# Gated linear attention by half chunks on 64x64 array tiles, ahead of a routed expert layer

## The chip, the cores and the metric

The kernel runs on one core of a Trainium2 chip. A core has a matrix engine (TensorE, PE in the profile; its weight loads are listed as PEld), three engines for elementwise work (VectorE or DVE, ScalarE or ACT, GpSimd or POOL), SyncE (SP), which issues DMA transfers, and 16 DMA engines behind it. The metric is the device time of the core in microseconds, the median of the runs. TensorE multiplies a stationary operand (`lhsT`, loaded as weights) with a moving one (`rhs`) and writes to PSUM[...].

## The reference

Two stages. The first is a gated linear recurrence over 768 steps, for 4 sequences of 8 heads with 48 dimensions each:

```python
for t in range(S):
    state = alpha[:, :, t, :, None] * state + np.einsum('bhd,bhe->bhde', k[:, :, t], v[:, :, t])
    y[:, :, t] = np.einsum('bhd,bhde->bhe', q[:, :, t], state)
```

Its result, as 3072 rows of 384 numbers, goes to a routed layer of 8 experts. Each row is given to the expert with the largest logit, and the result is scaled by that expert's softmax weight:

```python
logits = x @ w_gate                        # (3072, 384) @ (384, 8)
expert_idx = np.argmax(logits, axis=1)
...
h = np.maximum(x_sorted[lo:hi] @ w1[e], 0.0)   # w1[e]: (384, 1024)
y_sorted[lo:hi] = h @ w2[e]                    # w2[e]: (1024, 384)
...
return gate_w[:, None] * y
```

Everything is fp32.

## The kernel before

The recurrence is cut into 24 chunks of 128 steps (4 sequences of 6). Within a chunk the decays are turned into running sums of logarithms: with `cp = exp(cum)`, the queries become `q * cp`, the keys `k / cp`, and the chunk is a masked attention plus a product with the state that the chunk began with. Heads are handled in four pairs (`NP = 4`), each head padded from 48 to 64 (`DP`), so that a pair fills 128 partitions. A loop runs over `s`; in one pass different steps of several chunks are done:

```python
for s in range(-5, NT + 1):
    do(load, s + 8 if s + 8 >= 4 else -1, "akq")
    do(load, s + 5, "v")
    do(logs, s + 5)          # ScalarE: ln(alpha)
    do(cums, s + 4)          # TensorE: running sums; ScalarE: two exponentials
    do(operands, s + 3)      # GpSimd: k * icp, q * cp
    do(transposes, s + 2)
    ...
    do(rows, s - 1)
    do(scores, s + 1)
    do(keep_rows, s - 1)     # to the DRAM tensor x_rows
    do(decay_out, s + 3)
    do(decay_in, s + 2)
    ...                      # choice of experts for groups of chunks
    do(attend, s)
    ...                      # one-hot matrices of the routing
```

The steps that the change touches (cut):

```python
def cums(s):
    cum = ps.tile([C, Dm], F32, name="cum")
    nc.tensor.matmul(cum[:], lhsT=cmask[:], rhs=d["ln"][:], start=True, stop=True)
    ...
    nc.scalar.activation(d["icp"][:], cum[:], AF.Exp, scale=-1.0)
    nc.scalar.activation(d["cp"][:], cum[:], AF.Exp)

def decay_out(s):            # last row of cp to memory, and back as a column per head pair
    nc.scalar.dma_start(e_d[s : s + 1, :], st[s]["cp"][C - 1 : C, :])
def decay_in(s):
    for a in range(2):
        nc.scalar.dma_start(d["E"][a * DP : a * DP + D, :], ...)

def transposes(s):           # k and q, four 128x128 transposes each
    ...
        if i: nc.vector.tensor_copy(d[n][:], tp[:])      # qT
        else: nc.scalar.copy(d[n][:], tp[:])             # kT

def scores(s):
    for p in range(NP):
        for t, r in ((sA, 0), (sB, DP)):
            nc.tensor.matmul(t[:, p, :], lhsT=d["kT"][r : r + D, p, :], rhs=d["qT"][r : r + D, p, :], ...)
    nc.vector.tensor_tensor(d["dA"][:], sA[:], cmask..., op=ALU.mult)
    nc.scalar.copy(d["dB"][:], sB[:])
    nc.gpsimd.affine_select(d["dB"][:], d["dB"][:], ...)  # mask of the second head

def attend(s):
    y = ps.tile([C, NP, C], F32, name="y")
    if c > 0:                # state of the chunk before
        ... nc.tensor.matmul(y[r : r + DP, p, :], lhsT=st[s - 1]["U"][r : r + D, p, :], rhs=d["qT"][...], ...)
    for p in range(NP):
        for i, r in enumerate((0, DP)):
            nc.tensor.matmul(y[r : r + DP, p, :], lhsT=d["v"][:, 2 * p + i, :], rhs=d["d" + "AB"[i]][:, p, :], ...)
    if c + 1 < NB:           # k^T v of the chunk
        ... nc.tensor.matmul(kv[r : r + DP, p, :], lhsT=kqb[s % 4][:, 0, 2 * p + i, :], rhs=d["v"][...], ...)
    nc.vector.tensor_copy(d["yT"][:], y[:])
    # U = (kv + U before) * decay of the chunk: VectorE adds, GpSimd multiplies

def rows(s):                 # back to rows; `back` holds an identity and the gate's weights
    for p in range(NP):
        nc.tensor.matmul(xr[:, p, :], lhsT=d["yT"][:, p, :], rhs=back[:, p, :], start=True, stop=True)
    nc.vector.reduce_sum(lgn[:, s, :], ...)
def keep_rows(s):
    xs = work.tile([C, W], F32, name="xs")               # two buffers
    nc.scalar.copy(xs[:, :Dm]..., d["xr"][:, :, :D2])
    nc.gpsimd.tensor_copy(xs[:, Dm:], lgn[:, s, :])
    nc.sync.dma_start(x_d[s * C : (s + 1) * C, :], xs[:])
```

After the loop the last rows are routed, rows are gathered by expert from `x_rows`, and the expert layer runs (not changed but for the time at which weights are fetched). The weights of expert 0 are fetched in pass 15, those of experts 1 and 2 when the expert stage begins.

Of the kernel before, what the change touches and what calls it, by code (L numbers as in the profile page):

```python
# [8 lines left out]
F32 = mybir.dt.float32  # L9
# [9 lines left out]
def kernel(  # L19
# [10 lines left out]
):  # L30

# [42 lines left out]

    consts = ctx.enter_context(tc.tile_pool(name="consts", bufs=1))
    ident = consts.tile([C, C], F32)
    cmask = consts.tile([C, C], F32)
    back = consts.tile([C, NP, D2 + E], F32)
    kqb = [consts.tile([C, 2, H, DP], F32, name=f"kqb{i}") for i in range(4)]
    vb = [consts.tile([C, H, DP], F32, name=f"vb{i}") for i in range(6)]  # L80
    Ub = [consts.tile([C, NP, DP], F32, name=f"Ub{i}") for i in range(2)]
    Eb = [consts.tile([C, NP], F32, name=f"Eb{i}") for i in range(5)]

    def first_consts():
# [6 lines left out]
        for t in Ub + Eb:  # L91
            nc.vector.memset(t[:], 0.0)

        for a in range(2):
            r = slice(a * DP, a * DP + D)
            nc.vector.tensor_copy(
                back[r, :, a * D : (a + 1) * D], ident[r, None, a * DP : a * DP + D].to_broadcast([D, NP, D]),
            )
            nc.vector.tensor_scalar_mul(back[r, :, D2:], back[r, :, D2:], -1.0)
# [48 lines left out]
    e_d = nc.dram_tensor("decay_rows", (NT, Dm), F32, kind="Internal").ap()  # L148
# [27 lines left out]
    with tc.tile_pool(name="ld", bufs=6) as ld, \  # L176
         tc.tile_pool(name="work", bufs=2) as work, \
         tc.tile_pool(name="ps", bufs=1, space=PSUM) as ps, \
         tc.manual_schedule():
        st = {s: {} for s in range(NT)}  # L180

# [4 lines left out]
        def load(s, names):  # L186
            for n in names:
                src = rows_of({"a": alpha, "k": k, "q": q, "v": v}[n], s)
                if n == "v":
                    st[s][n] = vb[s % len(vb)]  # L190
                    nc.sync.dma_start(st[s][n][:, :, :D], src)
                else:
                    t = ld.tile([C, H, D], F32, name=n + "_sb", bufs=4 if n == "a" else 6)
                    nc.sync.dma_start(t[:], src)  # L194
                    st[s][n] = t
# [8 lines left out]
        def heads(t):  # L204
            return t[:].rearrange("s (h d) -> s h d", h=H)

        def cums(s):
            d = st[s]
            cum = ps.tile([C, Dm], F32, name="cum")
            nc.tensor.matmul(cum[:], lhsT=cmask[:], rhs=d["ln"][:], start=True, stop=True)  # L210
            d["icp"] = work.tile([C, Dm], F32, name="icp")
            d["cp"] = work.tile([C, Dm], F32, name="cp", bufs=3)
            nc.scalar.activation(d["icp"][:], cum[:], AF.Exp, scale=-1.0)  # L213
            nc.scalar.activation(d["cp"][:], cum[:], AF.Exp)  # L214

        def decay_out(s):
            if s % NB + 1 < NB:
                nc.scalar.dma_start(e_d[s : s + 1, :], st[s]["cp"][C - 1 : C, :])

        def decay_in(s):  # L220

            d = st[s]
            if s % NB + 1 < NB:
                d["E"] = Eb[s % len(Eb)]
                for a in range(2):
                    nc.scalar.dma_start(
                        d["E"][a * DP : a * DP + D, :], e_d[s].rearrange("(p a d) -> a d p", a=2, d=D)[a],
                    )

        def operands(s):  # L230
            d = st[s]
            kq = kqb[s % 4]
            nc.gpsimd.tensor_tensor(kq[:, 0, :, :D], d["k"][:], heads(d["icp"]), op=ALU.mult)  # L233
# [13 lines left out]

        def scores(s):
            d = st[s]
            sA = ps.tile([C, NP, C], F32, name="sA")  # L250
            sB = ps.tile([C, NP, C], F32, name="sB")
            for p in range(NP):
                for t, r in ((sA, 0), (sB, DP)):
# [12 lines left out]
        def attend(s):  # L266
# [38 lines left out]
            for r in ranked:  # L305
                slots_of(*r)
# [357 lines left out]
```

## Time and profile before

The time is 489.24 us (median of three; 489.02 to 489.99). The profiled execution spans 488.0 us.

| group (line) | count | mean ns | what it is |
|---|---|---|---|
| PE cum (210) | 48 | 601 | running sums, two records each |
| PE tp (241) | 192 | 282 | transposes |
| PE sA, sB (254) | 192 + 192 | 285 | scores |
| PE y (274) | 320 | 275 | product with the state |
| PE y (280) | 192 + 192 | 279 | product with the values |
| PE kvp (291) | 320 | 221 | k^T v |
| PE xr (313) | 192 | 275 | back to rows |
| DVE dA, yT, qT | 24 each | 687 to 689 | mask and copies out of PSUM |
| ACT kT, dB | 24 each | 591, 588 | copies out of PSUM |
| POOL kqb (233, 234) | 24 each | 996 | operands |
| POOL dB (261) | 24 | 634 | mask of the second head |

A row of the profile's groups names the line, the engine, the operation and the tiles (written <- read). For TensorE a second pair such as 128\*64 tells how many rows and columns of the array are used, followed by the moving operand. Matmuls overlap, so the mean length of one is longer than the distance between two; a rate is read from starts in the timeline. The expert stage's two groups of matmuls (lines 528 and 553) are busy for 148.4 and 146.8 us of the span.

### The profile page before, as it was taken

The page shows a single profiled execution, that of the slowest core. Times are in us where ns is not written, and L with a number is a line of the kernel's source. Part 1 is how long each engine was busy: PE and PEld are TensorE (multiplying, and loading weights), DVE is VectorE, ACT ScalarE, POOL GpSimd, SP SyncE. Part 2 cuts the span into 40 slices and gives each one's busy share as a digit, 9 for nine tenths or more (in the row PEclk, how much of TensorE's full clock was granted, in tenths as well). Part 3 has the DMA queues.
Part 4 walks back from the last instruction along what each step waited for, and adds up shares of the span by engine and source line. Part 5 has one row for each costly group of instructions (what it writes and reads, how often), then busy time and mean ns, then how long its engine had stood idle before and what let it go on. Part 6 is the DMA issues. An engine that isn't in the chain of part 4 may idle for free.

```text
span 488.0 us, 7370 instructions
## 1 busy us (share of the span) xinstructions
PE 457.6 (94%) x2881; PEld 297.4 (61%) x2881; DVE 142.3 (29%) x391; ACT 103.2 (21%) x209; POOL 137.8 (28%) x226
## 2 busy tenths in 40 slices
PE   2999999999999389999999999999999999999992
PEld 0788888888898275555555555555555455555451
DVE  2344766665778421212401201101201201301100
ACT  3544544544421001101001111011111001101010
POOL 3556745555642270010124010016020020010020
PEclk9999999999999779999999999999999999999997
DMA  9999999889992151300726400537300040000000
GB/s 161 199 177 203 207 210 203 168 170 272 299 356 107 50 160 39 142 32 8 267 75 211 135 32 0 189 118 249 129 28 16 1 166 22 1 20 16 2 32 25
DMA packets 127213, 59.76 MB, mean 122 GB/s; under 512 B 110304, under 2 KB 121604, under 8 KB 127178
## 3 DMA queue, kind: packets, MB, share of 16 engines
q1 hardware_dynamic: 114818, 48.87, 39.6%
q0 software_dynamic: 3584, 10.34, 6.4%
q10 hardware_dynamic: 8776, 0.08, 1.0%
q8 instruction: 23, 0.38, 0.3%
q14 instruction: 12, 0.10, 0.1%
HBM read 49.70 MB, written 10.35 MB: 123 GB/s over the span
## 4 chain that ended last, share of the span: by engine, by line
issue 54%; PE 27%; POOL 11%; DVE 2%; DMA 2%; SPq 1%; ACT 0%; POOLq 0%; ACTq 0%
POOL out_dram L559 6%; POOL xg L499 5%; PE sA L254 5%; PE y L280 4%; PE tp L241 4%; PE xr L313 4%; PE cum L210 4%; PE y L274 4%; PE kvp L291 2%; SPq L194 1%; DMA a_sb<-in_alpha_dram 1%; DMA x_rows<-xs 1%; DVE yT L295 1%; DVE sc L330 0%; DVE dA L258 0%
## 5 line engine op out<-in xcount | busy, mean ns | idle before, releaser
L528 PE MATMUL hp<-xT,w 128*128 128x448 f32 (+2 forms) x402 | 148.4, 530 | 1.2 <-DVE xT L524 1.2
L553 PE MATMUL zp<-w,h_sb 128*128 128x384 f32 (+1 forms) x512 | 146.8, 488 | 0.0
L528 PEld LDWEIGHTS hp<-xT,w 128*128 128x128 f32 x402 | 77.4, 194 | 69.9 <-issue 65.0
L553 PEld LDWEIGHTS zp<-w,h_sb 128*128 128x128 f32 (+1 forms) x512 | 81.1, 177 | 62.4 <-issue 13.6
L559 POOL DMA_INDIRECT out_dram<-zo,g_idx x28 | 27.7, 988 | 251.7 <-ACT zo L558 251.7
L542 DVE TENSOR_SCALAR h_sb<-hp 128x448 f32<-128x448 f32 x32 | 20.0, 624 | 218.4 <-PE hp L528 218.4
L544 ACT ACTIVATE h_sb<-hp 128x448 f32<-128x448 f32 x32 | 17.4, 543 | 142.0 <-PE hp L528 142.0
L558 ACT ACTIVATE zo<-zp,gw 128x384 f32<-128x384 f32 x28 | 16.3, 581 | 133.6 <-PE zp L553 129.0
L210 PE MATMUL cum<-ln,cmask 128*128 128x384 f32 x48 | 24.7, 601 | 8.7 <-ACT cp L214 4.4
L499 POOL DMA_INDIRECT xg<-x_rows,g_idx x28 | 26.9, 960 | 12.2 <-issue 12.2
L241 PEld LDWEIGHTS tp<-ident,kqb 128*128 128x128 f32 x192 | 23.5, 146 | 7.9 <-issue 4.2
L254 PE MATMUL sA<-qT,kT 48*128 48x128 f32 x192 | 27.7, 285 | 0.0
L254 PE MATMUL sB<-qT,kT 48*128 48x128 f32 x192 | 27.7, 285 | 0.0
L233 POOL TENSOR_TENSOR kqb<-k_sb,icp 128x384 f32<-128x384 f32 x24 | 23.9, 996 | 8.8 <-ACT icp L213 8.6
L241 PE MATMUL tp<-ident,kqb 128*128 128x128 f32 x192 | 26.2, 282 | 0.0
L280 PE MATMUL y<-dA,vb 128*64 128x128 f32 x192 | 26.1, 279 | 0.0
L280 PE MATMUL y<-dB,vb 128*64 128x128 f32 x192 | 26.1, 279 | 0.0
L313 PE MATMUL xr<-back,yT 128*128 128x104 f32 x192 | 25.4, 275 | 0.7 <-DVE yT L295 0.5
L261 POOL TENSOR_SCALAR_AFFINE_SELECT dB<-dB 128x512 f32<-128x512 f32 x24 | 15.2, 634 | 37.3 <-ACT dB L260 23.8
L254 PEld LDWEIGHTS sA<-qT,kT 48*128 48x128 f32 x192 | 23.1, 187 | 2.6 <-issue 0.3
L313 PEld LDWEIGHTS xr<-back,yT 128*128 128x128 f32 x192 | 23.3, 192 | 1.5 <-issue 1.0
L234 POOL TENSOR_TENSOR kqb<-q_sb,cp 128x384 f32<-128x384 f32 x24 | 23.9, 996 | 0.0
(117 smaller groups left out, 403.0 us busy)
## 6 DMA issues: line engine op xcount, KB each, us to landing
w<-in_moe_w_dram SPq DMA_DIRECT2D x16, 1536.0 KB, 6.8
x_rows<-xs SPq DMA_DIRECT2D x24, 196.0 KB, 2.9
a_sb<-in_alpha_dram SPq DMA_DIRECT2D x24, 192.0 KB, 4.1
k_sb<-in_k_dram SPq DMA_DIRECT2D x24, 192.0 KB, 3.8
q_sb<-in_q_dram SPq DMA_DIRECT2D x24, 192.0 KB, 4.0
vb<-in_v_dram SPq DMA_DIRECT2D x24, 192.0 KB, 4.6
Eb<-decay_rows ACTq DMA_DIRECT2D x40, 0.8 KB, 3.0
xg<-x_rows,g_idx POOLq DMA_INDIRECT x28, 3.1
```

The source lines that it names most:

```text
L210: nc.tensor.matmul(cum[:], lhsT=cmask[:], rhs=d["ln"][:], start=True, stop=True)
L233: nc.gpsimd.tensor_tensor(kq[:, 0, :, :D], d["k"][:], heads(d["icp"]), op=ALU.mult)
L234: nc.gpsimd.tensor_tensor(kq[:, 1, :, :D], d["q"][:], heads(d["cp"]), op=ALU.mult)
L241: nc.tensor.transpose(tp[:, p, :], pair(kqb[s % 4][:, i], p), ident[:])
L254: nc.tensor.matmul(t[:, p, :], lhsT=d["kT"][r : r + D, p, :], rhs=d["qT"][r : r + D, p, :], start=True, stop=True,)
L280: nc.tensor.matmul(y[r : r + DP, p, :], lhsT=d["v"][:, 2 * p + i, :], rhs=d["d" + "AB"[i]][:, p, :], start=(c == 0 and p == 0), stop=True, ...
L313: nc.tensor.matmul(xr[:, p, :], lhsT=d["yT"][:, p, :], rhs=back[:, p, :], start=True, stop=True)
L499: nc.gpsimd.indirect_dma_start(out=xg[:, j, :], out_offset=None, in_=x_d[:, :], in_offset=bass.IndirectOffsetOnAxis(ap=i, axis=0),)
L528: nc.tensor.matmul(hp[:, c0:c1], lhsT=w1[:, a, f * C : (f + 1) * C], rhs=xT[:, a, c0:c1], start=(a == 0), stop=(a == DB - 1), skip_group_c ...
L542: nc.vector.tensor_relu(h[:, f, :cols], hp[:, :cols])
L553: nc.tensor.matmul(zp[i * m : (i + 1) * m, :], lhsT=h[:, f, c0 : c0 + m], rhs=w2[:, f, :], start=(f == 0), stop=(f == FB - 1), skip_group_ ...
L559: ins = nc.gpsimd.indirect_dma_start(out=out[:, :], out_offset=bass.IndirectOffsetOnAxis(ap=idx, axis=0), in_=zo[:], in_offset=None, bound ...
```

## The change

The chunk stays at 128 steps, but inside it each half of 64 steps (`j`) is attended by itself: scores and value products exist only within a half, and what passes from half 0 to half 1 goes through an extra state, `U[:, 1]`. All products with operands of 48 or 64 rows and 64 columns are so placed that four of them, one for each half `j` and each head `a` of a pair, sit on the four 64x64 tiles of the array; for half 1 the two heads' places in `y` are exchanged (`at(j, a)`), so that state products on different rows never meet in the same PSUM partitions of a bank. The aim is to do four small products at a time where two larger ones were done, and to leave out the block of the score square that the mask sets to zero.

```diff
+    HALVES = [(j, a) for j in range(2) for a in range(2)]
+    def at(j, a):
+        return DP * (a ^ j)
...
+        def inter(s):
+            for p in range(NP):
+                for j, a in HALVES:
+                    if j or s % NB:
+                        nc.tensor.matmul(
+                            y_ps[at(j, a) : at(j, a) + DP, j, p, :],
+                            lhsT=Ub[s % 2][head(a), j, p, :], rhs=d["qT"][head(a), p, half(j)],
+                            start=(p == 0), stop=False, skip_group_check=True,
+                        )
         def scores(s):
-                for t, r in ((sA, 0), (sB, DP)):
+                for j, a in HALVES:
                     nc.tensor.matmul(
-                        t[:, p, :], lhsT=d["kT"][r : r + D, p, :], rhs=d["qT"][r : r + D, p, :], ...
+                        sc_ps[half(j), a, p, :], lhsT=d["kT"][head(a), p, half(j)], rhs=d["qT"][head(a), p, half(j)], ...
-            nc.scalar.copy(d["dB"][:], sB[:])
-            nc.gpsimd.affine_select(d["dB"][:], ...)
+            nc.vector.tensor_tensor(d["dAB"][:], sc_ps, m64..., op=ALU.mult)
         def attend(s):
+            n = s + 1            # kv of the next chunk, by halves
+                        nc.tensor.matmul(kv_ps[half(a), j, p, :],
+                            lhsT=kqb[n % 4][half(j), 0, 2 * p + a, :], rhs=st[n]["v"][half(j), 2 * p + a, :D], ...)
+                    nc.tensor.matmul(y_ps[at(j, a) : at(j, a) + DP, j, p, :],
+                        lhsT=d["v"][half(j), 2 * p + a, :], rhs=d["dAB"][half(j), a, p, :], ...)
+        def state(s):            # U[:, 1] = kv of half 0 + U[:, 0];  acc = kv of half 1 + U[:, 1]
+        def decay(s):            # GpSimd: U[:, 0] of the next chunk = acc * E
+        def results(s):
+            nc.scalar.copy(st[s]["yT"][:], y_ps)
         def rows(s):
-                nc.tensor.matmul(xr[:, p, :], lhsT=d["yT"][:, p, :], rhs=back[:, p, :], ...)
+                for j in range(2):
+                    nc.tensor.matmul(xr[half(j), p, :], lhsT=d["yT"][:, j, p, :], rhs=back[:, j, p, :], ...)
```

The chunk's decay is no longer sent through memory; TensorE picks the last row of `cp` out with a column of the identity, and ScalarE copies it:

```diff
-        def decay_out(s): / decay_in(s):     # three DMA issues by ScalarE
+        def decays(s):
+            last_ps = sums_tile()[:, Dm + 4 * E : Dm + 4 * E + NP]
+            for p in range(NP):
+                for a in range(2):
+                    nc.tensor.matmul(last_ps[half(a), p : p + 1],
+                        lhsT=cpb[s % 3][DP:, h : h + DP], rhs=ident[DP:, C - 1 :], ...)
+                nc.scalar.copy(st[s]["E"][:], last_ps)
```

The loop has a new order. The transposes come ahead of the running sums, the operands and logarithms one chunk further ahead of their use, and each PSUM bank is read by one engine at a time: scores and kv by VectorE, y by ScalarE. Loads go with a fixed lookahead and five buffers each for alpha, k and q; the store of rows stands at the head of the following pass.

```diff
+        for s in range(-5, NT):
+            do(store_rows, s - 1)
+            loads(s)             # v of s + 5, k and q of s + 7, alpha of s + 8
+            if s + 1 >= 0: attend(s)
+            do(state, s + 1)
+            ... decay(s + 1)
+            do(decays, s + 2)
+            do(results, s)
+            ... # ranking products
+            do(transposes, s + 2)
+            do(cums, s + 4)
+            do(operands, s + 4)
+            do(inter, s + 1)
+            do(scores, s + 2)
+            ... # one-hot matrices
+            do(rows, s)
+            do(keep_rows, s)
+            ... # choice of experts
+            do(logs, s + 5)
+            if s in (NT - 7, NT - 4):
+                e = (s - NT + 7) // 3
+                w_t[e] = fetch1(e), fetch2(e)
...
-        w_t[1] = fetch1(1), fetch2(1)      # at the start of the expert stage
```

So the weights of expert 0 are fetched in pass 17 and those of expert 1 in pass 20.

## The prediction

> **What bounds the kernel now.** I read the page first: the busy times and the slices.
>
> ```profile
> PE 457.6 (94%) x2881; PEld 297.4 (61%) x2881; DVE 142.3 (29%) x391; ACT 103.2 (21%) x209; POOL 137.8 (28%) x226
> ...
> PE   2999999999999389999999999999999999999992
> DMA  9999999889992151300726400537300040000000
> ```
>
> TensorE is full but for the start and one hole at slices 14 and 15. The hole is the border of two stages: attention up to about 164 us, the expert products from 170 us to the end. The diff touches the expert stage only in when weights are fetched, so its 318 us stay. What is to be won lies in the first 164 us, and there the DMA row is near 9 as well: a second resource stands close behind TensorE.
>
> Next the chain of waits in order of time, for one chunk in the middle. Columns: start, length (us), work.
>
> ```profile
> 65.65 0.84 PE cum L210 x2
> 66.50 0.87 PE tp L241 x8
> 67.37 0.87 PE xr L313 x8
> 69.33 1.02 PE y L274 x16
> 70.35 1.02 PE y L280 x16
> 71.83 0.84 PE cum L210 x2
> ```
>
> The chain never leaves TensorE: the period is 71.83 - 65.65 = 6.18 us. The scores fill 68.24 to 69.33 (1.09) and the key-value products 71.37 to 71.83 (0.46). The sum 0.84 + 0.87 + 0.87 + 1.09 + 1.02 + 1.02 + 0.46 is 6.17, so there is no idle time. The windows view of the same chunk agrees:
>
> ```profile
> 65.65:71.83 6.18, 6.18 (x84) 5.42 (x83) 4.39 (x14) 2.84 (x6) 3.23 (x6) 1.00 1.10 225
> ```
>
> PE is busy for all 6.18 us, VectorE for 4.39, ScalarE 2.84, GpSimd 3.23; the clock is full and DMA moves 225 GB/s. Then the timeline of TensorE by form, for what one product costs.
>
> ```profile
> 70.99 0.27 PE L280 MATMUL y<-dA,vb 128*64 128x128 f32 x1
> 71.00 0.27 PE L280 MATMUL y<-dB,vb 128*64 128x128 f32 x1
> 71.10 0.27 PE L280 MATMUL y<-dA,vb 128*64 128x128 f32 x1
> 71.11 0.27 PE L280 MATMUL y<-dB,vb 128*64 128x128 f32 x1
> 71.21 0.62 PE L291 MATMUL kvp<-vb,kqb 128*64 128x48 f32 x16
> 71.76 0.91 PE L210 MATMUL cum<-ln,cmask 128*128 128x384 f32 x2
> ```
>
> Every fp32 product is two records. Two products on different column halves start 0.01 us apart: they run together, and a round of two takes 0.11 us at 128 moving columns. Kvp (64 weight columns, 48 moving) has eight rounds: its 0.62 less the last record's 0.222 (median by the tile view), over seven gaps, is 0.057 us a round. So 64 weight columns with at most 64 moving ones cost about 0.058 a round; 128 of either cost 0.109 (0.87 / 8).
>
> Last, SyncE's issues, and the chain at the end of the stage.
>
> ```profile
> 39.06 0.64 SPq L322 DMA_DIRECT2D x_rows<-xs  x1
> ...
> 58.35 0.90 SPq L322 DMA_DIRECT2D x_rows<-xs  x1
> ```
>
> Between these lie three more stores and sixteen loads: four chunks in 19.29 us, 4.82 us a chunk, while SyncE still catches up with its lookahead. That is the pace at which loads and stores can go.
>
> ```profile
> 157.75 0.69 DVE yT L295
> ...
> 166.67 1.21 POOL xg L499
> ```
>
> The routing after the last chunk is a chain of short VectorE steps and a gather; the first expert matmul starts at 170.25.
>
> [...] the y groups take 1.02 for eight rounds of 0.109 = 0.87, so a switch is 0.15, for the scores 1.09 - 0.87 = 0.22. Four tiles at once occur in no part of this trace. [...] Loads here are runs of 48 floats, 192 B, and 4.82 us for 0.98 MB (four loads of 192 KB and a store of 196) is about 204 GB/s.
>
> **The change part by part, per chunk.** A round is up to four 64x64 products side by side; each group of 16 products has 4 x 2 = 8 rounds.
> - Scores: only keys and queries of the same half are multiplied; the block between the halves is left to the state. 8 x 0.058 = 0.46 for 1.09.
> - State products (inter): 0.46 for 1.02. They now also carry half 0 into half 1 through an extra state. y from scores: 0.46 for 1.02.
> - kv: by half chunks, 32 records for 16, four tiles for two: 0.46 as before.
> - Decays: new, eight products with one moving column, two tiles: 8 x 0.058 = 0.46 added. They replace the round trip of the decay row through memory.
> - rows: 64 weight columns, 104 moving, two tiles: 8 x 0.109 x 104/128 = 0.71 for 0.87.
> - Transposes 0.87 and sums 0.84 stay; transposes first merely give ScalarE and VectorE time for their copies.
> - Switches: 64x64 to full, to 64x64, to 128x64, to 64x64: 0.15 + 0.22 + 0.15 + 0.15 = 0.67. About 0.2 of the sums' 0.84 (two passes over 384 columns at 0.109 per 128 are 0.65) was their own switch and goes.
>
> Sum: 5 x 0.46 + 0.71 + 0.87 + 0.65 + 0.67 = 5.2 us; 5.3 with the ranking products. Before, the first chunk of a sequence saved its whole state product and the last its kv; now the first still runs one half and the last one half, in as many rounds, so these shortcuts are gone. The y groups on lines 274 and 280 put chunk 0 at 21.75 and chunk 18 at 129.98, hence 6.01 a chunk on average. 18 x (6.01 - 5.3) = 12.8 us. The last five chunks took 26.6 (to 156.6); without sums, then without transposes and scores, I give them 5.3 + 5.3 + 4.5 + 4.5 + 3.2 = 22.8: 3.8 us.
>
> Other engines: ScalarE loses the dB copy (0.59) and three DMA issues (0.31 to 0.46 each), gains the yT copy (0.59) and a tiny decay copy (I take 0.2): ln 0.52, exps 0.97, kT 0.59, yT 0.59, xs 0.48, decay 0.2 are 3.4 of 5.3. VectorE loses yT (0.69), gains a 0.35 add: about 4. GpSimd loses the select (0.63). None gets to 5.3, so these changes by themselves lie beside TensorE.
>
> Start: the products of chunk 0 come in the pass that also needs alpha of chunk 4, the 15th load in the new order: 0.8 + 15 x 1.03 us a load (37 loads stood ahead of the store at 39.06) is 16.3, so I put y of chunk 0 near 17, 4.7 earlier than 21.75; ScalarE now takes the next logarithm after the exponentials, not before, and no longer stalls them on a later load. Against this stands the result buffer xs with its two copies: xs of chunk 2 needs the first store landed. That store now has 31 loads ahead of it: 0.8 + 31 x 1.03 = 32.7, plus 2.9 to land (the page's median), about 35.6. TensorE alone would want it near 17 + 3 x 5.3 = 33, so some 2.6 are lost again. Net 2 us gained. 12.8 + 3.8 + 2 = 18.6 for the stage. The routing tail keeps its length, and expert 1's weights no longer compete with the first gather: up to 0.5 us, within the error.
>
> 489.2 - 18.6 is 470.6; I put 470.
>
> **Rivals.**
> (a) Four tiles do not run at once, or TensorE's instruction stream doesn't keep up: records per chunk double from 82 to about 170. Against it: pairs start 0.01 apart and two kinds of pairs, rows and columns, both work. For it: nothing here shows more than two. If kv, y, inter and scores ran two by two, 4 x 0.46 is added: 7.1 us a chunk, 18 x 1.1 and the rest 25 us slower: about 512.
> (b) DMA becomes the bound. It needs 4.82 a chunk against 5.3, and two experts' weights (3 MB each, 3.15 MB at about 400 GB/s, some 8 us) are now pulled into the stage, against one before. They come after the last k, q and alpha loads, so I expect little; but if chunk periods stretched to 5.8, it is about 479.
> (c) ScalarE's order: kT waits behind the decay copy and yT, the next exps behind kT. Its chain inside a chunk (decays end at 1.4, then 0.2, 0.6, 0.6 and about 0.2 of latency: 3.0) is ahead of the scores (due at 3.6) by 0.6 only. If it slips, the period is 5.6 to 5.8: 475 to 479.
> (d) All goes faster: cheaper switches, no wait for xs; 5.0 a chunk, but DMA's 4.82 stops it: about 462.
>
> **Range and chances.** (d) gives the lower end with some margin, 460; (b) and (c) the upper, 481. Faster by over 2% means under 479.5. I give (a) in full or in part 9%, and 7% to a gain eaten by waits; faster 0.84.
>
> **What would show it.** Windows of one chunk: period near 5.3 and PE busy throughout. The timeline: four starts within 0.03 us, rounds of 0.058; rounds of 0.11 mean (a). The chain of waits staying on PE, else ACT kT, Eb or xs (c), or loads of alpha and x_rows (b). First y near 17 us, last near 138, expert start about 151, expert stage still 318 us. It is wrong if the four-tile rounds cost over 0.09 us, or if the expert stage moves.

## The result, and the profile after

| | median us (range, runs) | ratio to the kernel before, 95% interval |
|---|---|---|
| before | 489.18 (489.02 to 489.99) | |
| after | 505.92 (505.64 to 507.32, 4) | 1.0345 (1.0322 to 1.0367) |

The change makes the kernel 16.7 us slower; 19 us faster were predicted. The ratio leaves out executions over 1.5% above the fastest of their kernel, which the medians keep. First the page of the kernel after: busy times, the slices of TensorE, its clock and DMA, and the queue that the page lists as `instruction`.

```profile
PE 456.9 (90%) x4993; PEld 292.3 (58%) x4993; DVE 131.7 (26%) x396; ACT 106.3 (21%) x229; POOL 126.6 (25%) x206
...
PE   3899898989869649999999999999999999999993
...
PEclk9999988989989777999999999999999999999997
DMA  9999977979764925130255330255330040000000
...
q8 instruction: 40, 0.66, 0.6%
```

The same queue in the page of before (packets, MB, share):

```profile
q8 instruction: 23, 0.38, 0.3%
```

TensorE is busy for as long as before (456.9 us against 457.6) in a span that is 17.6 us longer. Where its row of before had nines, several slices of the attention stage have an 8 or a 6 now, and the clock row falls to 8 or 7 in five slices of that stage and in two behind its last y; before, it did so only at the border of the stages. (At the start the clock row has nines because the trace has no record of the clock there, not because the clock was full; see below.) Records of matrix products, two to an fp32 product, went from 2881 to 4993. The line of queue 8 was easily passed over: 40 packets of instructions for 23.

Two passes in the windows view of after. Columns: stretch, length, then busy time and count of PE, PEld, VectorE, ScalarE and GpSimd, the granted clock, the DMA share and GB/s.

```profile
70.40:75.57 5.17, 5.17 (x184) 4.39 (x180) 2.65 (x5) 2.94 (x7) 2.44 (x4) 1.00 0.58 128
75.57:84.16 8.59, 6.83 (x185) 5.53 (x180) 4.13 (x16) 2.95 (x8) 3.78 (x10) 0.80 0.90 159
```

The first is the pass that was predicted: 5.17 us, TensorE busy throughout, full clock. The next one has about the same work for TensorE (185 records for 184), takes 8.59 us, leaves TensorE idle for 1.76 and drops to a mean clock of 0.80. TensorE's timeline shows two kinds of waits. Columns: start, length, work, and in brackets the idle time before it and what ended it.

```profile
62.49 0.28 PE L242 MATMUL cum<-ident,cpb 64*64 64x1 f32 x5
64.24 0.51 PE L242 MATMUL cum<-ident,cpb 64*64 64x1 f32 x11 [1.47 <-issue]
...
75.07 0.68 PE L313 MATMUL scp<-vb,kqb 64*64 64x48 f32 x32
75.57 0.66 PE L323 MATMUL y<-dAB,vb 64*64 64x64 f32 x32
76.06 0.58 PE L242 MATMUL cum<-ident,cpb 64*64 64x1 f32 x16
78.41 0.18 PE L397 MATMUL cum<-ohs,ones_sq 128*128 128x32 f16 x1 [1.76 <-POOL ohs L392]
...
144.29 0.66 PE L323 MATMUL y<-dAB,vb 64*64 64x64 f32 x30
148.29 0.37 PE L323 MATMUL y<-dAB,vb 64*64 64x64 f32 x1 [3.34 <-issue]
```

The 32 records of key-value products take 0.50 us (75.07 to 75.57) and the 32 of value products 0.49: the four tiles do run at once. But the decay products at 62.49 stop after five of sixteen and go on 1.47 us later, and the value products at 144.29 stop after thirty of 32 for 3.34 us. Their operands lie in the same tiles as those of the records just done; "issue" says that the profile shows nothing they waited for. And at 78.41 the ranking products of the routing wait for GpSimd. The waits view of after, for TensorE (what waited, for what: us in total, times, longest):

```profile
PE cum L397 <- POOL ohs L392: 6.8, 5, 1.8
...
PE y L323 <- issue: 3.9, 2, 3.3
PE y L286 <- issue: 3.8, 3, 1.6
...
PE cum L242 <- issue: 1.5, 1, 1.5
```

"Issue" lies on several lines with different work, so it isn't one instruction's fault. I therefore counted TensorE's instructions in the order of the trace: matrix products, weight loads, semaphores and a few others, 5898 before and 10145 after. This is worked out from the trace of after: from the first to the last y (value products), the ten holes that are no wait for a semaphore. A hole is the distance from one start to the next; the first column is the place in that order at which it stands:

```
instruction   193 + 256 x   hole us, ends at   last packet of instructions
1217           4            0.74   41.0        38.47 to 39.65
1473           5            0.78   45.3        42.37 to 43.82
1729           6            0.31   50.0        47.46 to 48.42
2497           9            1.66   64.2        61.33 to 62.71
4289          16            0.40   98.5        95.58 to 96.96
5569          21            0.82  121.1        118.57 to 119.74
6593          25            1.41  142.0        139.65 to 140.57
6849          26            3.55  148.3        145.87 to 146.95
7617          29            1.29  165.5        163.21 to 164.16
7873          30            1.79  171.9        169.44 to 170.47
sum                        12.8
```

Every one stands at the same place in a block of 256 instructions (other starts over 0.6 us apart without a semaphore are those around a sum of 384 columns at half clock), and work goes on 1.34 to 1.54 us after the end of a packet of queue 8. The packets are 16,384 bytes (0.66 MB / 40); 17 more of them than before make 4352 instructions at 256 to a packet, and TensorE has 4247 more. From these counts I read, as an inference, that TensorE's instructions come by this queue, 256 in a packet, and that at a border TensorE waits until the next packet is there. In the attention stage of before, the packet ends 5 to 9 us ahead of the border that the same count gives, and no hole stands at a border. In after, ten of the 30 borders from the first to the last y have a hole.

The chain of waits of after shows a third thing, at the same eight transposes:

```profile
18.88 1.90 PE tp L261 x8
...
71.49 1.03 PE tp L261 x8
```

At the start 1.90 us stand for 1.03, which I take for half clock until the first records of the clock, all at full, begin (31.3 us in this execution; in before, 17.2). Between the first and the last y the kernel after has 26.6 us of half clock: 5.6 before that first rise and 21.0 in stretches that begin in a hole or a wait or less than 1.3 us behind it, at a granted clock of 0.50 (65.4 to 68.9, 79.1 to 82.5, 103.0 to 106.4, 147.4 to 154.2, 171.3 to 178.1); before has none there. Not each wait has such a stretch: after the ranking waits that ended at 52.7 and 128.0 us (1.0 and 1.7 us) the clock stayed full. In the second pass above, the wait (1.76 us) and what the half clock behind it adds (an estimate: half of the 3.41 us from 79.1 to 82.5) come to about the 3.42 us by which the pass is longer.

### The profile page after: what moved, and what is told of

Read it like the earlier page. It is cut to its first block, busy times and chain, and to the rows that moved or that the text cites. A ratio compares the mean times of both kernels' runs of the same rounds, so it can differ in the third digit from the quotient of the medians.

```text
span 505.6 us, 11587 instructions
## 1 busy us (share of the span) xinstructions
PE 456.9 (90%) x4993; PEld 292.3 (58%) x4993; DVE 131.7 (26%) x396; ACT 106.3 (21%) x229; POOL 126.6 (25%) x206
## 4 chain that ended last, share of the span: by engine, by line
issue 54%; PE 26%; POOL 9%; DVE 5%; DMA 3%; SPq 1%; ACT 1%; POOLq 0%; ACTq 0%
POOL out_dram L629 5%; PE tp L261 5%; PE cum L225 4%; PE y L286 3%; PE xr L356 3%; POOL xg L569 3%; PE scp L296 3%; PE scp L313 2%; PE cum L242 2%; PE y L323 2%; PE hp L598 1%; DVE dAB L301 1%; DMA out_dram<-zo,g_idx 1%; DVE oh_r L420 1%; DMA a_sb<-in_alpha_dram 1%
## 5 line engine op out<-in xcount | busy, mean ns | idle before, releaser
L623 PEld LDWEIGHTS zp<-w,h_sb 128*128 128x128 f32 (+1 forms) x512 | 81.1, 177 | 62.3 <-issue 13.6
L614 ACT ACTIVATE h_sb<-hp 128x448 f32<-128x448 f32 x32 | 17.4, 543 | 140.9 <-PE hp L598 140.9
L261 PE MATMUL tp<-ident,kqb 128*128 128x128 f32 x192 | 31.0, 312 | 1.2 <-issue 1.2
L286 PEld LDWEIGHTS y<-qT,Ub 48*64 48x64 f32 x704 | 16.2, 155 | 19.8 <-issue 14.9
L264 DVE COPY qT<-tp 128x512 f32<-128x512 f32 x24 | 16.6, 692 | 40.1 <-PE tp L261 40.1
L301 DVE TENSOR_TENSOR dAB<-scp,m 128x512 f32<-128x512 f32 x24 | 16.6, 691 | 37.0 <-PE scp L296 37.0
L286 PE MATMUL y<-qT,Ub 48*64 48x64 f32 x704 | 20.3, 248 | 4.2 <-issue 3.8
L254 POOL TENSOR_TENSOR kqb<-q_sb,cpb 128x384 f32<-128x384 f32 x24 | 24.0, 1000 | 0.0
L366 ACT COPY xs<-xr 128x384 f32<-128x384 f32 x24 | 11.5, 479 | 57.7 <-DVE lgn L361 42.2
L356 PE MATMUL xr<-back,yT 128*64 128x104 f32 x384 | 23.4, 264 | 0.1
L594 DVE COPY xT<-xtp 128x384 f32<-128x384 f32 (+1 forms) x32 | 14.8, 503 | 26.8 <-PE xtp L592 26.8
L323 PE MATMUL y<-dAB,vb 64*64 64x64 f32 x768 | 18.0, 229 | 3.9 <-issue 3.9
```

The source lines that it names most:

```text
L254: nc.gpsimd.tensor_tensor(kq[:, 1, :, :D], d["q"][:], heads(d["cp"]), op=ALU.mult)
L261: nc.tensor.transpose(tp[:, p, :], pair(kqb[s % 4][:, i], p), ident[:])
L286: nc.tensor.matmul(y_ps[at(j, a) : at(j, a) + DP, j, p, :], lhsT=Ub[s % 2][head(a), j, p, :], rhs=d["qT"][head(a), p, half(j)], start=(p = ...
L301: nc.vector.tensor_tensor(d["dAB"][:], sc_ps, m64[:, None, None, :].to_broadcast([C, 2, NP, DP]), op=ALU.mult,)
L323: nc.tensor.matmul(y_ps[at(j, a) : at(j, a) + DP, j, p, :], lhsT=d["v"][half(j), 2 * p + a, :], rhs=d["dAB"][half(j), a, p, :], start=(p = ...
L356: nc.tensor.matmul(xr[half(j), p, :], lhsT=d["yT"][:, j, p, :], rhs=back[:, j, p, :], start=True, stop=True, skip_group_check=True,)
```

## The experiments

All are edits of the kernel after unless the name begins with `before`. "Against before" is the difference of the medians beside runs of the kernel before on the same chip; for the change itself it is +16.7. The ratio of rank_later stands on three of its four executions, that of rank_later_few_loads on 13 of 18; by it these two are 14.2 us above and 0.7 us below the kernel before. "Holes" is the sum of holes at block borders, "ranking" that of TensorE's waits ahead of ranking products, the last groups behind the last y included, "half" the half clock between first and last y, all from one profiled execution.

| run | us (range, runs) | against before | ratio, 95% | holes | ranking | half |
|---|---|---|---|---|---|---|
| after | 505.92 | +16.7 | 1.0345 (1.0322 to 1.0367) | 12.8 | 10.6 | 26.6 |
| rank_later | 506.27 (500.90 to 508.54, 4) | +15.9 | 1.0289 (1.0223 to 1.0355) | 23.8 | 5.8 | 14.5 |
| warm_start | 505.56 (503.68 to 507.20, 4) | +15.2 | 1.0322 (1.0304 to 1.0340) | 16.3 | 8.6 | 18.1 |
| decay_dma | 498.86 (497.77 to 502.05, 4) | +8.5 | 1.0185 (1.0143 to 1.0228) | 14.2 | 10.7 | 18.1 |
| few_loads | 495.65 (493.88 to 497.42, 2) | +5.3 | 1.0109 (1.0067 to 1.0151) | 9.0 | 10.7 | 14.8 |
| rank_later_few_loads | 492.19 (486.06 to 495.33, 18) | +1.3 | 0.9986 (0.9962 to 1.0011) | 7.0 | 4.7 | 16.3 |
| decay_dma_rank_later | 496.09 (493.05 to 499.46, 4) | +6.7 | 1.0144 (1.0074 to 1.0214) | 25.0 | 3.9 | 8.4 |
| wide_quarter | 488.46 (485.67 to 492.53, 12) | -0.7 | 0.9997 (0.9976 to 1.0017) | 0 | 15.7 | 13.7 |
| wide_rank_later | 482.57 (477.44 to 483.64, 4) | -6.6 | 0.9837 (0.9791 to 0.9882) | 0 | 8.9 | 12.3 |
| before_logs_last | 501.13 (498.52 to 502.34, 6) | +10.2 | 1.0203 (1.0174 to 1.0232) | | | 7.2 |
| before_fill | 491.21 (490.27 to 493.96, 22) | +0.3 | 1.0011 (1.0000 to 1.0022) | | | 0 |
| before_state_full | 494.40 (492.89 to 495.96, 6) | +5.3 | 1.0112 (1.0089 to 1.0134) | | | 0 |

The theory at the outset: the time is lost to the supply of instructions. Its rivals: the wait for the ranking, the half clock at the start, the order of the logarithms.

**rank_later: is it the ranking wait?** Groups that end before chunk 16 are ranked one pass later, so that GpSimd is done.

```diff
-   for g in groups_of if g[-1] == s - 1
+   for g in groups_of if g[-1] == (s - 2 if g[-1] < 16 else s - 1)
```

> The ranking products of the first four groups of chunks come one pass later, so that the counts they need from GpSimd are long there. Theory 1 (each wait costs itself [...], so that a window of 3.41 us at half clock follows): the waits of 1.2 to 1.95 us (6.6 in all) go and at least two of the three single half-clock windows between 60 and 120 us go with them: 494 to 497 us. Rival (small 64x64 products lower the clock by themselves): only the waits go, the half-clock windows stay in number: 499 to 501 us. If TensorE would wait there for instructions anyway: 503 to 506 us.

Measured: +15.9 for +16.7, within the scatter of the four runs and close to the third of the outcomes named. The ranking waits shrank from 10.6 to 5.8 us and the holes grew from 12.8 to 23.8. The profiled execution was the longest of the four, so 23.8 may be on the high side; but decay_dma_rank_later below, profiled in the shortest of its four, shows the same growth. TensorE's waits for issue in this kernel:

```profile
PE y L323 <- issue: 7.3, 5, 3.4
...
PE y L286 <- issue: 5.8, 4, 2.1
...
PE cum L242 <- issue: 3.5, 2, 2.3
```

Line 323 stood at 3.9 and line 286 at 3.8 before this edit. The reading that fits: a wait for GpSimd gives the next block of instructions time to come; without that wait, TensorE reaches the border earlier and waits there. The waits don't add up: this one is real, and no gain from taking it away is clear of the scatter as long as the supply is short.

**warm_start: is it the half clock at the start?** Full-size products on a constant tile stand ahead of the first pass and in the passes -4 and -3.

```diff
+   filler(320); filler(320)          # 128x128 weights, fp32, result never read
    for s in range(-5, NT):
        ...
+       if s in (-4, -3): filler(384 if s == -4 else 192)
```

> Filler products of full size (128 weight columns, 192 to 384 moving columns) are put in the holes of TensorE before 11 us; nothing reads their result. Theory 1 (the late rise of the clock, at 31 us instead of 17 us, is what delays the first chunks): the clock is full by about 18 us, the first value products start near 20 instead of 25.7 us, 499 to 501 us. Rival ([...]): the clock rises at 28 to 31 us again, 505 to 507 us.

Measured: the clock was full from 15.7 us, the first y at 22.0 instead of 25.7, and yet +15.2 by the medians. Holes were 16.3. That the fillers raised the clock isn't shown: rank_later has no fillers, and there the clock was full from 15.7 us and the first y at 22.0 too. Nor was the earlier start lost in the profiled execution, the shortest of the four: its last y comes at 169.5 us for 174.3, and it took 503.68 us where the profiled execution of after took 507.32. How the other three started isn't on record. So the start can be worth some 4 us of a single execution, but not the 16.7.

**decay_dma: fewer instructions, nothing left out.** The decays go through memory again, as before; TensorE has 308 instructions a chunk instead of 340.

```diff
-   for p, a: nc.tensor.matmul(last_ps[half(a), p : p + 1], lhsT=cpb[...], rhs=ident[DP:, C - 1 :], ...)
-   nc.scalar.copy(st[s]["E"][:], last_ps)
+   do(decay_out, s + 3); do(decay_in, s + 2)      # after the scores, three DMA issues by ScalarE
```

> The decays go through memory again as in the kernel before; the eight products a chunk with one moving column and the ScalarE copy are gone. Theory 1 (TensorE's instruction stream is a bound: 32 of some 330 instructions a chunk go[...]): period of an undisturbed chunk 4.7 us, stalls at the borders of 256 instructions fall from 12 to about 5 us in all, fewer half-clock windows: 486 to 492 us. Rival (the instruction stream is not a bound, only the products' 0.5 us count): 24 x 0.5 = 12, 493 to 495 us. Rival 2 (the round trip makes the state late): waits for the decay appear, 503 us or more.

Measured: +8.5, 8.2 us less than the change. The best pass takes 4.73 us, not 5.14, and the first y is at 19.0 (clock full from 11.6), 6.6 us earlier than in after. The holes remain (14.2): the passes became shorter too. A new wait came in, seen in the waits of this kernel between 20 and 140 us, GpSimd for the decay from memory:

```profile
POOL Ub L334 <- DMA Eb<-decay_rows: 18.7, 8, 5.8
```

So the run doesn't part the supply from the work of the decay products themselves, and it met neither the 486 to 492 us of the theory nor its 5 us of holes; what it shows is that these products didn't pay for their place.

**few_loads: do the loads hold up the instructions?** Chunks from 5 (v: from 6) on use the data of earlier chunks, so three quarters of the loads aren't made; the output is that of other data.

```diff
+   if n == "v" and s >= len(vb): st[s][n] = vb[s % len(vb)]
+   elif n != "v" and s >= AHEAD + 1: st[s][n] = st[s - AHEAD - 1][n]
```

> After the first five chunks (six of v) nothing is loaded: later chunks use the early chunks' k, q, alpha and v again, so the output is of other data; the stores of rows and all weight fetches stay. Theory 1 (TensorE stalls at every 256th instruction because the fetch of the next block queues behind the small-packet loads): the stalls between 36 and 135 us nearly vanish, from 5 us to under 1.5 us, and with them a half-clock window: about 498 us. Rival (the fetch has a fixed latency of some 4 us that the denser stream now runs into): the stalls stay, over 3.5 us in the same stretch: 503 to 506 us.

Measured: +5.3, 11.4 us less than the change, with every instruction kept. Holes fell from 12.8 to 9.0 us; of those that stayed, 6.0 are at 133 us and later, where the weights are still fetched. Between 36 and 135 us they fell from 4.7 to 3.1, not under the 1.5 expected. So holes are 3.8 of the 11.4 us; the first y also comes 3.8 us earlier (clock full from 15.4 us for 31.3), and half clock falls from 26.6 to 14.8. Loads did lie on the path, though TensorE's waits of after name no load; that they did so through the fetch alone isn't shown.

**stream_alone: the supply by itself.** A kernel of nothing but 64x64 fp32 products with the operands at rest, four to a round, in three stretches: with no DMA, beside 56 loads as the recurrence has them, beside weights. Nothing of the reference is computed; the time (137.76) means nothing.

```python
quads(40); touch(x[0][:, 0, :], D)
for s in range(14):
    for t in (k, q, v, alpha): nc.sync.dma_start(x[i % 12][:], rows_of(t, s)); i += 1
quads(30)          # 16 products of 64x64, moving 64, by 30
```

> Nothing of the reference is computed: TensorE runs three stretches of groups of sixteen 64x64 products (64 instructions a group, no waits inside), the first with no DMA, the second beside 192 KB loads in runs of 192 B, the third beside weight loads. Theory (the instruction fetch bounds the dense stream): already in the first stretch the groups take more than the 0.50 us they take between stalls in the attention; a block of 256 instructions takes 3.5 to 4.5 us for 2.0 us of work, longer in the second stretch and longest in the third, with all holes at one residue modulo 256. Rival (only DMA load delays the fetch): the first stretch runs at 2.0 to 2.2 us a block without holes. For the clock: if small products starve it by themselves, it stays at half in the first stretch beyond 15 us.

Its timeline of TensorE, three blocks without DMA and three beside the loads (a record is half a product, with a weight load of its own, so 128 records are 256 instructions):

```profile
25.63 2.09 PE L76 MATMUL y<-mv,st 64*64 64x64 f32 x128 [1.36 <-issue]
29.09 2.09 PE L76 MATMUL y<-mv,st 64*64 64x64 f32 x128 [1.36 <-issue]
32.54 2.09 PE L76 MATMUL y<-mv,st 64*64 64x64 f32 x128 [1.36 <-issue]
...
39.45 2.09 PE L76 MATMUL y<-mv,st 64*64 64x64 f32 x128 [0.86 <-issue]
43.73 2.09 PE L76 MATMUL y<-mv,st 64*64 64x64 f32 x128 [2.19 <-issue]
48.28 2.99 PE L76 MATMUL y<-mv,st 64*64 64x64 f32 x128 [2.46 <-issue]
```

With no DMA at all, a block of 256 instructions is worked off in 2.09 us and the next one starts 3.45 us after it (29.09 to 32.54): 1.36 us of every block are waiting (1.64 in the three blocks ahead of those shown, 3.73 apart). The 3.45 are made up of about 1.1 us from the border to the start of the next packet of queue 8, 0.9 to 1.1 us for the packet, and 1.3 to 1.4 until work goes on. Beside loads the distance is 4.28 and 4.55 here, 4.0 to 4.8 in the whole stretch, 4.3 on average. Two windows of the same run, without DMA and beside the loads (busy time of PE, PEld, VectorE and GpSimd, clock, DMA share, GB/s):

```profile
20.00:37.00 17.00, 9.91 (x590) 9.12 (x578) 0.00 (x0) 0.00 (x0) 1.00 0.01 4
41.00:66.00 25.00, 13.51 (x684) 12.66 (x674) 0.00 (x0) 0.00 (x0) 0.86 0.88 172
```

A chunk of the kernel after has 340 instructions: 340 / 256 x 3.45 = 4.6 us where DMA is idle, and x 4.3 = 5.7 beside loads. Between the two lies the 5.15 us that TensorE needs for a chunk's work. So, by this estimate, the change is bound by TensorE where the queue is quiet and by the supply where it isn't; few_loads agrees. A block that follows a wait can come sooner: behind the ranking wait at 78.4 us in the trace of after, two borders are 3.1 us apart (81.4 and 84.6), and the packet between them had started at 80.6, ahead of the first of the two. The third stretch didn't reach the weights while it ran; what they do to a fetch by themselves stays unmeasured.

**wide_quarter: the same columns in fewer instructions.** Each group of sixteen 64x64 products becomes four with 256 moving columns (kv: 192), all with the first pair's weights: 148 instructions a chunk, tiles, modes and columns as in the kernel after. The output isn't the reference's.

```diff
-   for p in range(NP):
-       for j, a in HALVES:
-           nc.tensor.matmul(sc_ps[half(j), a, p, :], lhsT=d["kT"][head(a), p, half(j)], rhs=d["qT"][head(a), p, half(j)], ...)
+   for j, a in HALVES:
+       nc.tensor.matmul(sc_ps[half(j), a, :, :], lhsT=d["kT"][head(a), 0, half(j)], rhs=d["qT"][head(a), 0:2, :], ...)
    # likewise inter, y and kv
```

> The changed kernel with each group of sixteen 64x64 products (64 instructions) replaced by four on the same tiles with 256 (192 for kv) moving columns: the same columns stream through the array, with the same waits and readers, but with the first pair's stationary operand for all pairs, so the output is not the reference's. Some 340 instructions a chunk become about 148. Theory (the instruction stream is the bound): no holes at block borders before the weights are fetched (12.8 us gone), a period of 4.7 to 4.9 us where 5.15 was the best, fewer half-clock windows; the ranking waits (6 to 7 us) remain: last value products near 148 instead of 175 us, 478 to 482 us. Rival (holes and lowered clock come from the waits and the DMA load, whatever the count of instructions): last value products later than 162 us, 493 us or more.

Measured: -0.7, 17.4 us less than the change, and not one hole at a block border. Not all of the 17.4 is the supply: the passes are shorter as well, 4.91 us for 5.17 (the key-value group, for one, takes 0.37 us for 0.50, with a quarter of the weight loads), in this kernel's timeline from one key-value group to the next:

```profile
30.75 0.56 PE L310 MATMUL scp<-vb,kqb 64*64 64x192 f32 x8
...
35.66 0.56 PE L310 MATMUL scp<-vb,kqb 64*64 64x192 f32 x8
```

Over 23 passes 0.26 is at most 6 us. And the first y comes at 21.3 us for 25.7, with the clock full from 15.1 for 31.3, as in some runs that keep all instructions. So, as an estimate, the supply itself is worth between 7 us (17.4 - 6 - 4.4) and 17.4; the holes alone were 12.8. I had expected 478 to 482; what took the difference back is in the waits of the same kernel:

```profile
PE cum L393 <- POOL ohs L388: 9.1, 5, 2.3
```

6.8 in the kernel after became 9.1, and all waits ahead of ranking products 15.7 for 10.6: the mirror of rank_later. Four of its passes took 8.65 to 8.99 us.

**wide_rank_later: the ranking wait where the supply is no limit.** The edit of rank_later on top of wide_quarter.

> The same with the ranking products one pass later. With instructions no longer scarce, taking the ranking waits away must now pay, other than in the kernel as changed (where 506 stayed 506): 6 us less than the run before it, 472 to 476 us, hardly a half-clock window before 130 us. Rival (the waits only move elsewhere): the same time as the run before it within 2 us.

Measured: -6.6, 5.9 us below wide_quarter (the 6 expected, though not the 472 to 476), from the edit that was worth 0.8 in the kernel after. The same line of its waits:

```profile
PE cum L393 <- POOL ohs L388: 3.2, 2, 2.1
```

Half clock behind the clock's first rise went from 13.7 to 6.8 us with it; but that rise came at 30.8 us in this execution, for 15.1, so that the whole is 12.3. This pair against after and rank_later, with the holes that grew there, is the evidence that the two waits stand in for each other.

**rank_later_few_loads and decay_dma_rank_later** add the same edit to few_loads and to decay_dma.

> Both the later ranking and the missing loads (later chunks use early chunks' data, output of other data). Theory (waits for the ranking and holes at the instruction blocks stand in for each other, and the loads only lengthen the fetch): ranking waits of the first four groups gone, holes at the block borders up from 9.0 to 12 us or more, 492 to 496 us. Rival (independent costs): 6.6 us less than with few loads alone, and its half-clock windows: 485 to 488 us.

> Decays through memory and the later ranking together, nothing left out: 308 instructions a chunk. Theory (the instruction stream is the bound at 4.0 to 4.6 us a block of 256 beside loads: 308 / 256 x 4.3 = 5.2 us a chunk): the ranking waits are given back in part at the block borders, as in the later ranking alone, but less: 493 to 497 us, between the decays through memory alone (498.9) and the kernel before. Rival (the two changes add up freely): 6 us and a clock window or two less than the decays alone: 488 to 491 us.

Measured: 4.0 us less than few_loads (6.0 by the ratios), and 1.8 less than decay_dma with holes grown from 14.2 to 25.0. In rank_later_few_loads the holes did not grow to the 12 us expected but fell from 9.0 to 7.0: with the loads gone, the ranking waits were not given back at the borders. The more room the supply has, the more the edit brings: 0.8 (340 instructions, all loads), 1.8 (308, all loads), 4.0 (340, few loads), 5.9 (148). The first two lie within the scatter of their runs, few_loads has two runs only, and by the ratios the four are 2.7, 2.0, 6.0 and 7.8; so only the last two gains are clear of the scatter. Of kernels that leave nothing out, decay_dma_rank_later is the best form of the change that I ran, and still 6.7 us behind the kernel before.

**before_logs_last: the order of the logarithms.** In the kernel before, the next logarithm goes to the end of the pass, as in the change.

```diff
-   do(logs, s + 5)      # ahead of cums
    ...
+   do(logs, s + 5)      # end of the pass
```

> The kernel before, with the logarithms at the end of a pass as in the changed kernel, so that the exponentials no longer stand behind a logarithm that waits for its load. If the order of ScalarE's work made the start late: first value products near 19 instead of 21.75 us, 486.5 to 488 us. Rival (the start is bound by TensorE at half clock): no change, 489 us.

Measured: +10.2, first y at 24.4 for 21.7 and 7.2 us of half clock in the stage. I had taken this order for a gain at the start. By itself it is a loss in the kernel before; what it does in the kernel after, with other lookaheads, wasn't tried.

**before_state_full: what does a switch of the array's tiling cost?** In the kernel before, the state product is made with four full 128x128 weights (the state block by block on the diagonal), right after the products to rows, so that one switch to 64 rows and back goes.

```diff
-   nc.tensor.matmul(y[r : r + DP, p, :], lhsT=U[r : r + D, p, :], rhs=d["qT"][r : r + D, p, :], ...)   # two per pair
+   nc.tensor.matmul(y[:, p, :], lhsT=U[:, p, :], rhs=d["qT"][:, p, :], ...)                            # one per pair
```

> The kernel before, with the product of the state done by four full 128x128 products on a block-diagonal state, beside the transposes and rows products, instead of eight 64x64 ones between two other tilings: as long in array time (0.87 us), one switch of tiling and 16 instructions fewer a chunk. If a switch is worth the 0.15 us of the prediction: 20 chunks, 3 us less: 485.5 to 487 us. Rival (the two extra half-size operations on VectorE and GpSimd make the state late, or the switch is hidden): 489 us or more.

Measured: the undisturbed pass takes 6.07 us for 6.18, so the switch, with the 16 instructions, is 0.11, near the 0.15 I used. The kernel is slower all the same (+5.3): single passes take 6.76 and 7.63, and the last five chunks 30.1 us for 26.7. U is needed earlier in the pass, but TensorE's waits for it come to 1.1 us between 40 and 140; what else makes it slower isn't shown.

**before_fill: half clock at the border of the stages.** Nine full-size products between routing and gather in the kernel before.

```diff
+   fill = ps.tile([C, NP, C], F32, name="sA")
+   for _ in range(2): filler(256)          # after the last one-hot matrices
+   for _ in range(7): filler(NP * (D2 + E))
```

> The kernel before, with nine filler products in TensorE's hole between the routing and the first gathered rows (158 to 170 us); nothing reads them. Theory ([...]): the half clock from 164 to 178 us shrinks or goes, the first expert products run at full clock, 3 to 4 us are saved: 485 to 486.5 us. Rival (the clock falls for another reason, or fillers delay the gathered rows' transposes): 488.5 us or more.

Measured: half clock at this border fell from 13.65 to 3.41 us and the time stayed (+0.3). From 170 to 190 us TensorE is busy for 16.4 us instead of 18.5: what the products gained at full clock went into waits. So half clock cost nothing here.

## Why the prediction was wrong, step by step

- **Four tiles at once, rounds of 0.058 us: right.** 32 key-value records in 0.50, 32 value records in 0.49: about 0.062 a round. The undisturbed pass takes 5.14 to 5.17, a little under the 5.2 of the sum.
- **Switches of 0.15: about right** (0.11 measured for one).
- **The step that failed: "a round is up to four 64x64 products side by side; each group of 16 products has 4 x 2 = 8 rounds", taken as the whole cost of a group.** It is the array's cost. A group also has 64 instructions, and these have a pace of their own: in a steady stream 3.45 us for 256 with DMA idle, 4.0 to 4.8 beside loads. Rival (a) named it ("TensorE's instruction stream doesn't keep up: records per chunk double from 82 to about 170"), but I argued only against its other half: that pairs start 0.01 us apart shows that two tiles run together, not that instructions arrive. The 9% were also put on a figure, 512, that came from tiles two by two. The page had a hint: 23 packets of 16 KB by queue 8. In the stage before, a block lasts 256 / 164 x 6.18 = 9.6 us; with 340 instructions in 5.2 us it lasts 3.9. In the trace of before a packet alone takes 0.9 to 1.5 us, and none had been asked for at that rate. The two signs of being wrong that I had named, rounds over 0.09 us and an expert stage that moves, both stayed away: they tested the array's cost alone.
- **"None gets to 5.3, so these changes by themselves lie beside TensorE": wrong by order, not by sums.** GpSimd and VectorE have time to spare, but the choice of experts ends a pass and the ranking products head the next, so TensorE waits 1.0 to 1.8 us four times in mid-stage (6.8 us in the waits view, with a fifth near the end). I had counted 0.1 a chunk for their work and no wait.
- **18 x (6.01 - 5.3): wrong.** From chunk 0 (25.7) to chunk 18 (137.3) a chunk takes 6.20 on average, 0.9 above 5.3: 13.6 us more than predicted for this stretch, with the 2.6 that I allowed for the first store.
- **The last five chunks at 22.8: 37.0** (137.3 to 174.3). The longest hole (3.55) is here: its packet started 3.9 us after the border before, while DMA moved mostly weights (2.4 MB from 140 to 150 us); that the weights held it up is likely, not shown. In all, 8.0 us of the holes and two stretches of 6.83 us at half clock (from 147.4 and 171.3) are in these chunks.
- **"y of chunk 0 near 17": 25.7.** The 15th load wasn't what came last. From 8.2 us on the chain of waits stays on TensorE at half clock and on short steps between its products. In other runs of this layout the first y came at 19.0, 21.3 and 25.3 with the clock rising at 11.6, 15.1 and 30.8: it follows the clock, which I had taken as full. Why the clock rises so late in some executions isn't shown.
- **"Two experts' weights are pulled into the stage, against one before": wrong in the "before".** In the trace of before, all six weight transfers are issued from 113.8 to 137.6 us, within the stage, ahead of TensorE's own progress.
- **The expert stage stays 318 us: right**, 317.9 after, 317.75 before. **Rival (b)**, DMA as the bound, was right in a way I hadn't meant: beside loads a block of instructions came every 4.3 us on average, without DMA every 3.45 (stream_alone). **Rival (c)**: kT, yT and the decay copy are in none of TensorE's long waits between the first and the last y (the largest is 0.3 us, for the decay).

The three misses of the stage, 8.7 us at the start, 13.6 to chunk 18 and 14.2 in the last five chunks, make 36.5, the last y being at 174.3 for 137.8, and the time missed by 35.9. As an estimate for the 27.8 from the first y on: holes 12.8, ranking waits 6.8 and up to 12 for half clock (26.6 us, with 1.90 for 1.03), less 3.5 because an undisturbed pass takes 5.15 and not 5.3, is 28. Where a hole lies inside a stretch of half clock, this counts it twice, so that the sum comes so near is partly luck.

In the sum: from +16.7, removing the surplus of instructions gives -0.7 and moving the ranking in addition -6.6. The prediction was -19. Of the 12.6 left (482.6 for 470), 8.3 lie ahead of the first y in wide_rank_later (25.3 for 17) and about 4 after it. Which part of those is half clock and which the ranking waits that remain at the end of the stage (8.9 us in all) was not separated, and whether a form with few instructions and the reference's own output exists wasn't tried.

## What to carry to other kernels

Before cutting products into smaller ones, count instructions as well as array time: each fp32 product is four of them here (two records of the product and two of its weight loads), and in a steady stream a block of 256 came no faster than every 3.45 us, and every 4.0 to 4.8 us beside loads. Small tiles did pay here once the moving operand was long (wide_rank_later, whose output isn't the reference's). And two waits on one path can replace each other: an edit without a clear gain beside a tighter limit (0.8 us) was worth 5.9 once that limit was gone, so try such edits again after each removal.

## What the runs showed that I had not expected

- **Instructions came more slowly than TensorE took them for dense small products.** In stream_alone it took 256 in 2.09 us, 8.2 ns each, and waited 1.36 us for the next 256, with DMA at a share of 0.01; beside loads it waited up to 2.73.
- **The clock fell after some short waits and not after others.** In after, idle times of TensorE of 1.47, 1.76 and 1.38 us (ended at 64.2, 78.4 and 102.8 us) were each followed by 3.41 us at a granted clock of 0.50 (from 65.4, 79.1 and 103.0); one of 1.71 us (ended at 128.0) wasn't. In stream_alone, waits of 1.36 to 1.64 us in each block left the clock full (1.00) from 8.2 to 37 us, and it first fell at 49.2, after waits of 2.19 and 2.46 (shown above). What decides it, these runs don't show.
